# Key features of two token tiles by way of an SBUF copy, a third nested product in one mixing group, and new engine orders

## The chip, the cores and the metric

The kernel runs on one core of a Trainium2 chip. The metric is device time in microseconds (us) of one execution. Engines: TensorE (PE), which multiplies matrices; VectorE (DVE); ScalarE (ACT); GpSimd (POOL); SyncE (SP), which issues most of the DMA transfers. PE takes its operands from SBUF and writes PSUM, eight banks of 128 partitions x 512 fp32.

## The reference

The input is x of 2048 tokens x 512. The first part is linear attention over 32 heads of 16, the second a gated MLP with a spatial product over the tokens (F = 1792, Fh = 896):

```python
def _A_ref(x, wqkv, wo):
    qkv = ...            # x @ wqkv, split into 32 heads
    q, k, v = (qkv[0], qkv[1], qkv[2])
    phi = lambda t: jnp.where(t > 0, t + 1, jnp.exp(t)) + 1e-06
    pq, pk = (phi(q), phi(k))
    kv = jnp.einsum('bhsd,bhse->bhde', pk, v)
    z = jnp.einsum('bhsd->bhd', pk)
    num = jnp.einsum('bhqd,bhde->bhqe', pq, kv)
    den = jnp.einsum('bhqd,bhd->bhq', pq, z)[..., None] + 1e-06
    ...                  # (num / den) @ wo

def _B_ref(x, w_in, w_sp, b_sp, w_out):
    z = _gelu(jnp.einsum('bsd,df->bsf', x, w_in))
    z1 = z[..., :Fh].copy()
    z2 = _layernorm(z[..., Fh:], axis=-1)
    g = jnp.einsum('ts,bsf->btf', w_sp, z2) + b_sp[None, :, None]
    return jnp.einsum('bsf,fd->bsd', z1 * g, w_out)

h = x + _A_ref(_layernorm(x, axis=-1), A_wqkv, A_wo)
h2 = h + _B_ref(_layernorm(h, axis=-1), B_w_in, B_w_sp, B_b_sp, B_w_out)
```

## The kernel before

**Tiles and stages.** The 2048 tokens are 16 tiles of 128 rows. In the head (0 to about 46 us) each tile of x is normalised: BATCH_NORM statistics and their aggregation on DVE (L535, L536), or for tile 1 two accumulating passes on ACT; 1/sqrt(variance) by ACT (tiles 0, 2, 3) or POOL; then xn (L580 on DVE, L583 on ACT). For the first six tiles PE transposes xn (four transposes, L594) and ACT copies the result to xnT; the others are transposed by DMA. Four 512-wide matmuls by the key part of wqkv then give the keys of a tile in a PSUM bank, `phi` (L601) makes the key features pk, and L684 accumulates pk against xn over all tiles in four banks. From that sum follow the matrix m (cast at L794), and with the query features pqT the denominator (L817), its reciprocal r on ACT, the spread of r over partitions by DMA on SP (L808, `spread`), the multiply of pqT by r (L833), and the products pqT x m that give h (L845). Then come the second layer norm, w_in with gelu, the spatial mixing with w_sp, the gate and w_out.

**phi** takes exp of the keys on ACT (e), min and add on DVE (L606), and ends in one of two ways. Without `split` a DVE scalar_tensor_tensor (L611) reads PSUM: max(t + 1 + eps, e). With `split`, ACT copies t + 1 + eps to the destination in SBUF (bf16), and a DVE tensor_tensor (L609) takes the maximum there in place. For the keys, `k_unit` (L640) asks for each tile i below SINGLE = 4 whether i is in KSPLIT, and for later pairs whether their first tile is.

**The mixing.** All large products are in Strassen-Winograd form: w_sp and z2 are cut into 2 x 2 blocks, and sums of blocks take the place of an eighth of the products. `mix(ia, ib, nest)` (L1060) does two pairs of token tiles, (ia, ia + 8) and (ib, ib + 8), over one half of the features, 448 wide (HW). The four calls take the tiles of MIX = (0, 1, 2, 3, 7, 4, 5, 6) two by two; the third has the tiles 7/15 and 4/12. Set c uses the PSUM banks B = SETS[c], A = B + 1 and E = B + 2, with SETS = (0, 3); the banks 6 and 7 are left for other work, in this stage for `mo_pair`. `gate` (L1006) finishes a piece: ACT adds the bias out of PSUM into u (L1011), DVE multiplies z1 by u in place (L1012). `gate_p` (L1020) does it when a part p was set aside earlier: DVE adds PSUM and p into u (L1023), then multiplies (L1024). When a tile is finished, SP issues a transposing DMA of z1 to zgT, named zg and the tile number, which w_out needs.

**A nested product** (`nested`, L1035) takes a further level of the same scheme for both pairs of a group together: seven products of four matmuls, 224 wide (HQ), in two banks, with four sums u of the weight's quarters (L748, `comb`), four sums v of the other operand's quarters (`quarter_sums`, L1028), two adds of a piece p into PSUM (L1044) and four 224-wide copies on ACT (L1045). The same operand takes 2 x 8 matmuls of 448 without it. NEST gives each of the four groups a number: bit 1 nests the first product, bit 2 the product of q1 with zt1. The first group has neither, the others have both.

**w_out.** `mo_pair` (L1130) does it for two tiles, again in Strassen form, in two banks (6 and 7 for all but the last pair): sums us of zgT (L748), matmuls, adds of h into tmp (L1147) and the final adds into h (L1159), then a store. The last two tiles go through `mo` (L1122, add at L1127). `mo_pair(0)` runs from 139.9 us, between the second and third group's matmuls.

**Order.** Nothing is scheduled at run time. ORDER is a packed list of the numbers of all operations (1256), and each engine runs its own in that order and waits for semaphores where an operation depends on another engine or on a DMA. So an operation that has to wait holds everything that stands behind it on its engine. Buffers are placed by hand at byte offsets, and two tiles may share an address when their uses don't overlap; the dependencies include those.

Of the kernel before, what the change touches and what calls it, by code (L numbers as in the profile page):

```python
# [252 lines left out]
def bass_sequential_preLN__linear_attn_block__mixer_gmlp__prompt_kernel(  # L253
# [14 lines left out]
    H = 32  # L268
# [151 lines left out]
    def matmuls(out_ap, pairs, start=True, stop=True, onto=False, **k):  # L420
        n = out_ap.free_size() if callable(getattr(out_ap, "free_size", None)) else out_ap.shape[-1]

        kw = {"skip_group_check": True} if onto else {}

        def fn(pe):
            inst = None
            for i, (a, b) in enumerate(pairs):
                inst = pe.matmul(out_ap, lhsT=a, rhs=b, start=start and i == 0, stop=stop and i == len(pairs) - 1, **kw)  # L428
            return inst
        return PE(fn, [a for p in pairs for a in p], [out_ap], len(pairs) * max(65.0, n / 2.4 + 2.5), **k)  # L430
# [437 lines left out]
    def half(b):  # L868
        return bank(b, HW)
# [150 lines left out]
    def gate_p(n, c, b, p):  # L1020
        o, u = z1[n][:, c], u_t[cnt[0] % len(u_t)]
        cnt[0] += 1
        dve(lambda v: v.tensor_tensor(u, half(b), p, ALU.add), [half(b), p], [u], HW, ps=True)  # L1023
        dve(lambda v: v.tensor_tensor(o, u, o, ALU.mult), [u, o], [o], HW, acc=2)  # L1024
# [35 lines left out]
    def mix(ia, ib, nest, early=False):  # L1060
        ss = range(HT)
        sa = [[sae[0], sae[1]], [sae[2], sa_[1][1]]] if early else sa_
        sets = ((ia, 0), (ib, 1))
        Y = {}
        for i, c in sets:
            Y[i] = blocks(i)
        if nest & 1:
            nested(SETS[0] + 1, SETS[1] + 1, wt[ia][:, 0:HT, :], wt[ib][:, 0:HT, :], z2[:, 0:HT, lo], nu1, nv1, np1)
        for i, c in sets:
            B, A, E = SETS[c], SETS[c] + 1, SETS[c] + 2  # L1070
            y11, y21, y12, y22 = Y[i]
# [91 lines left out]
        load_w(n)  # L1163
    MIX = (0, 1, 2, 3, 7, 4, 5, 6)
    for k in range(0, HT, 2):
        mix(MIX[k], MIX[k + 1], NEST[k // 2], k == 0)
        if k == 0:
            for q in ZLATE:
                cell2(q, win1, wq1[0], 6, 7, p5z[q % 2], z1_half)
            load_wout()  # L1170
            for n in W4:
                load_w(n)
            if any(m & 1 for m in NEST):
                quarter_sums(nv1, z2[:, 0:HT, lo])
            if any(m & 2 for m in NEST):
                quarter_sums(nv5, zt1)
# [44 lines left out]
```

## Time and profile before

| | us |
|---|---|
| median of 3 executions (224.97 to 225.69) | 225.41 |
| the profiled execution | 225.59 |
| its span in the profile | 223.6 |
| PE busy, 1318 matmuls | 217.5 |
| DVE busy, 440 instructions | 191.3 |
| ACT busy, 271 instructions | 138.6 |
| POOL busy, 133 instructions | 46.6 |
| HBM read and written | 6.95 MB and 2.10 MB |

Busy times overlap; what matters is which engine the others wait for. The chain of waits is followed back from the last instruction, at each step to whatever released it. By its lines, 82% of the span is matmuls of L428, which is the helper for nearly all of them, and 6% those of L684. A group's line gives count, busy time and the mean of one; an instruction's time contains its start and drain, so a matmul's record overlaps the next one's, and the step from start to start is shorter than its duration. Line 2 of the page shows how full each of 40 slices of the span is; POOL is empty from the middle on:

```profile
PE   7799999998999999999999999999999999999995
DVE  3899778899999999999999998999695976694666
ACT  5587844469898999999674456624353434526130
POOL 2445400000279465637710000000000000000000
```

### The profile page before, as it was taken

The numbers are of one execution on the slowest core, as the hardware profiler recorded it, in microseconds if no ns is written. First come the engines' busy times: TensorE is split into PE (matmuls) and PEld (weight loads), VectorE is DVE, ScalarE is ACT, GpSimd is POOL, SyncE is SP. The second block draws the span as 40 slices with busy tenths as digits, with TensorE's granted clock in tenths as the row PEclk, the third lists the DMA queues.
The fourth block names the chain that finished last, engine by engine and source line by source line (L and its number), as shares of the span: only waits on it lengthen the run. The fifth ranks groups of instructions, "written<-read, shape, count | busy, mean of one in ns | idle before, by whom it ended". The sixth has DMA issues, their size and how long they took to land.

```text
span 223.6 us, 3752 instructions
## 1 busy us (share of the span) xinstructions
PE 217.5 (97%) x1318; PEld 121.6 (54%) x1318; DVE 191.3 (86%) x440; ACT 138.6 (62%) x271; POOL 46.6 (21%) x133
## 2 busy tenths in 40 slices
PE   7799999998999999999999999999999999999995
PEld 7344444443434545445555555767776658666664
DVE  3899778899999999999999998999695976694666
ACT  5587844469898999999674456624353434526130
POOL 2445400000279465637710000000000000000000
DMA  5664999977752359840843344998444208204444
GB/s 187 205 197 93 170 221 250 197 178 169 164 132 56 70 104 132 121 93 0 109 85 129 77 85 80 171 178 132 82 100 85 58 12 166 42 1 89 107 134 142
DMA packets 73938, 26.85 MB, mean 120 GB/s; under 512 B 63680, under 2 KB 73920, under 8 KB 73920
## 3 DMA queue, kind: packets, MB, share of 16 engines
q1 hardware_dynamic: 73216, 26.03, 56.7%
q10 hardware_dynamic: 704, 0.59, 0.8%
q8 instruction: 10, 0.16, 0.3%
q14 instruction: 8, 0.07, 0.1%
HBM read 6.95 MB, written 2.10 MB: 40 GB/s over the span
## 4 chain that ended last, share of the span: by engine, by line
PE 90%; DMA 4%; ACT 2%; DVE 2%; SPq 1%; ACTq 0%; issue 0%; DVEq 0%
PE psum L428 82%; PE psum L684 6%; DMA wqkv<-in_A_wqkv_dram 3%; DMA r<-rcp 1%; ACT ct L447 1%; DVE h L1159 1%; SPq L808 1%; DVE pqT L833 1%; PE psum L706 0%; PE psum L594 0%; ACTq L458 0%; DVE m L794 0%; ACT psum L447 0%; ACT r L447 0%; ACT z1t L447 0%
## 5 line engine op out<-in xcount | busy, mean ns | idle before, releaser
L447 ACT ACTIVATE psum<-psum 128x448 f32<-128x448 f32 (+2 forms) x67 | 28.0, 432 | 31.0 <-PE psum L428 24.3
L428 PE MATMUL psum<-z,wt 128*128 128x448 bf16 (+1 forms) x232 | 46.4, 343 | 0.1
L428 PEld LDWEIGHTS psum<-z,wt 128*128 128x128 bf16 x232 | 22.6, 98 | 17.7 <-ACT np L447 0.4
L428 PE MATMUL psum<-win,hnT 128*128 128x448 bf16 x112 | 25.8, 353 | 0.0
L447 ACT ACTIVATE e<-psum 128x1024 bf16<-128x1024 f32 (+1 forms) x18 | 16.7, 932 | 13.5 <-PE psum L428 13.5
L447 ACT ACTIVATE z1t<-psum 128x448 bf16<-128x448 f32 (+1 forms) x24 | 15.9, 669 | 4.6 <-PE psum L428 2.9
L428 PE MATMUL psum<-ws,hs 128*128 128x448 bf16 x72 | 18.7, 353 | 0.0
L447 ACT ACTIVATE p<-psum,b 128x448 f32<-128x448 f32 x16 | 9.8, 634 | 11.8 <-PE psum L428 9.7
L428 PEld LDWEIGHTS psum<-win,hnT 128*128 128x128 bf16 x112 | 10.7, 98 | 10.5 <-DMA hnT<-hn 0.4
L1023 DVE TENSOR_TENSOR u<-psum,p 128x448 bf16<-128x448 f32 x16 | 9.9, 621 | 7.5 <-PE psum L428 7.5
L428 PE MATMUL psum<-zt,sa 128*128 128x448 bf16 (+1 forms) x92 | 16.3, 316 | 0.0
L447 ACT ACTIVATE u<-psum,b 128x448 bf16<-128x448 f32 x16 | 10.1, 632 | 10.0 <-PE psum L428 8.8
L875 DVE TENSOR_TENSOR psum<-psum,p5z 128x448 f32<-128x448 f32 x24 | 14.9, 626 | 1.4 <-ACT z1t L447 0.4
L428 PE MATMUL psum<-wqkv,xnT 128*128 128x512 bf16 x64 | 15.3, 379 | 0.3 <-DMA wqkv<-in_A_wqkv_dram 0.2
L428 PE MATMUL psum<-xnT,wqkv 128*128 128x512 bf16 x64 | 15.3, 379 | 0.0
L684 PE MATMUL psum<-pk,xn 128*128 128x512 bf16 x64 | 15.3, 379 | 0.0
L428 PE MATMUL psum<-wout,zgT 128*128 128x256 bf16 (+1 forms) x77 | 15.1, 302 | 0.0
L428 PE MATMUL psum<-m,pqT 128*128 128x512 bf16 x64 | 14.7, 380 | 0.1
L447 ACT ACTIVATE z<-psum 128x896 bf16<-128x896 f32 x16 | 14.7, 918 | 0.1
L428 PE MATMUL psum<-zt,wt 128*128 128x448 bf16 x64 | 13.4, 352 | 0.0
L535 DVE BATCH_NORM_STATS2 st<-x 128x6 f32<-128x512 bf16 x15 | 9.8, 682 | 3.4 <-DMA x<-in_A_x_dram 3.3
L559 POOL TENSOR_SCALAR st<-st 128x1 f32<-128x1 f32 x10 | 3.7, 374 | 40.8 <-ACT sh L447 36.7
(153 smaller groups left out, 435.2 us busy)
## 6 DMA issues: line engine op xcount, KB each, us to landing
r<-rcp SPq DMA_DIRECT2D x16, 128.0 KB, 2.7
out_dram<-h SPq DMA_DIRECT2D x15, 128.0 KB, 1.8
win<-in_B_w_in_dram SPq DMA_DIRECT2D x4, 448.0 KB, 4.3
x<-in_A_x_dram SPq DMA_DIRECT2D x6, 256.0 KB, 4.3
wqkv<-in_A_wqkv_dram SPq DMA_DIRECT2D x2, 512.0 KB, 5.5
wout<-in_B_w_out_dram SPq DMA_DIRECT2D x1, 896.0 KB, 5.0
wt<-in_B_w_sp_dram SPq DMA_TRANSPOSE x32, 4.4
wo<-in_A_wo_dram SPq DMA_DIRECT2D x1, 512.0 KB, 4.6
```

Source lines behind the costliest of these rows:

```text
L428: inst = pe.matmul(out_ap, lhsT=a, rhs=b, start=start and i == 0, stop=stop and i == len(pairs) - 1, **kw)
L447: return g.add("ACT", lambda ac: ac.activation(out_ap, in_ap, func, **kw), [in_ap, *extra], [out_ap] + ([accum] if accum is not None else []),
L535: dve(lambda v: v.bn_stats(s[:, 0:6], src[:, n, :]), [src[:, n, :]], [s[:, 0:6]], D)
L559: pool(lambda p: p.tensor_scalar(s[:, 2:3], s[:, 0:1], s[:, 0:1], -1.0 / (n * n), op0=ALU.mult, op1=ALU.mult), [s[:, 0:1]], [s[:, 2:3]], 240)
L684: inst = pe.matmul(bank(CB[c]), lhsT=xn[:, i, c * P:(c + 1) * P], rhs=pk[:, i, :], start=i == 0, stop=i == NT - 1)
L808: g.add("SP", lambda q: q.dma_start(dst, src_ap), [rcp[:, i:i + w, :]], [dst], cost=700, lat=2200, dma=f"r{tg}{c // 2}")
L833: dve(lambda v, q=q, r=r: v.tensor_tensor(q, q, r, ALU.mult), [q, r], [q], 2 * GW, acc=2)
L875: dve(lambda v: v.tensor_tensor(half(b), half(src), p, ALU.add), [half(src), p], [half(b)], HW, ps=True)
L1023: dve(lambda v: v.tensor_tensor(u, half(b), p, ALU.add), [half(b), p], [u], HW, ps=True)
L1159: dve(lambda v, o=o, q=q, add=add: v.tensor_tensor(o, q, add, ALU.add), [q, add], [o], DH2, ps=True)
```

## The change

It does three things.

1. KSPLIT goes from empty to (0, 2): by the test in `k_unit`, tiles 0 and 2 take the `split` branch of `phi`. Each has one more ACT pass (PSUM to pk, 512 wide), and its DVE operation reads two bf16 tiles in SBUF instead of PSUM.
2. NEST goes from (0, 3, 3, 3) to (0, 3, 7, 3). Bit 4, new, nests a third product in the third group: the lower block of w_sp's row of `tl` by the second half of z2. It runs in the banks 6 and 7, and its results are gated from there with `gate_p`, with p2 copied out of bank A by ACT. Sums of z2's quarters (nv2) are made ahead of the group. The new buffers share addresses: nv2 with z1 of the tiles 2, 3, 10 and 11, nu2 and p2 with the tails of the w_sp rows 2, 10, 3 and 11.
3. ORDER is new, with 1279 operations. In the head, PE's transposes of the tiles 3 and 1 stand ahead of the first product by wqkv instead of behind it; ACT's second pass over tile 1 stands ahead of the first rstd pass, and DVE aggregates the tiles 2 and 3 ahead of the first xn. Between 18 and 40 us some loads change places on SP. In each of the first r spreads two issues change places, so that the part the first multiply waits for comes second of four. From about 139 us to the end, the order on PE, DVE, ACT and SP is new: `mo_pair(0)` starts behind the third nested product; the last two products of the last but one pair, and the order of transposes and stores on SP, change at the end.

```diff
-ORDER = "c-jTQ1Aq_!5Cp*8z00=o*)~7hwryLV`)u2`ZQHhO*9;I5kwC;pI7CJi7(&A#L`5`&L3G4J2qZuf#6Uvi...
+ORDER = "c-jTQ1Aq_!5Cp)z-OIM|*)~7hwryLV`)u2`ZQHhO*9;I5kzk0A(1?sE2nQh~98nPs;SmPW5f4NNBtR0xKt...
...
+    o_ur = [o_wsp + n * S * 2 + ZR for n in (2, HT + 2, 3, HT + 3)]
+    nv2 = [g.sbuf(f"nv2{k}", o_xnT + slot[n] * ZR, [HT // 2, HW // 2], BF16) for k, n in enumerate((2, 3, HT + 2, HT + 3))]
+    nu2 = [g.sbuf(f"nu2{k}", o_ur[k // 2] + k % 2 * (S // 2), [HT // 2, P], BF16) for k in range(4)]
+    p2 = [g.sbuf(f"p2{c}", o_ur[2 + c], [HW], FP32) for c in (0, 1)]
+    assert N4 <= ZR and ZR + S <= S * 2
...
-    QSPLIT, KSPLIT, CACT = (6, 7), (), 2
+    QSPLIT, KSPLIT, CACT = (6, 7), (0, 2), 2
...
-    NEST = (0, 3, 3, 3)
+    NEST = (0, 3, 7, 3)
...
             matmuls(half(B), [(q2[:, s, :], zt2[:, s, :]) for s in ss], **onto)
-            matmuls(half(A), [(wt[tl][:, HT + s, :], z2[:, HT + s, lo]) for s in ss], **onto)
-            gate(tl, lo, A)
+            if nest & 4:
+                act(p2[c], half(A), ACT.Identity, HW, bias=b32[:, tl:tl + 1], extra=[b32[:, tl:tl + 1]])
+                if c == 0:
+                    nested(6, 7, wt[ia][:, HT:NT, :], wt[ib][:, HT:NT, :], z2[:, HT:NT, lo], nu2, nv2, np1)
+                gate_p(tl, lo, 6 + c, p2[c])
+            else:
+                matmuls(half(A), [(wt[tl][:, HT + s, :], z2[:, HT + s, lo]) for s in ss], **onto)
+                gate(tl, lo, A)
...
     for k in range(0, HT, 2):
+        if NEST[k // 2] & 4 and not NEST[k // 2 - 1] & 4:
+            quarter_sums(nv2, z2[:, HT:NT, lo])
         mix(MIX[k], MIX[k + 1], NEST[k // 2], k == 0)
```

More of the change, by code (lines that the diff above doesn't have):

```diff
@@ L15 @@
 SEM_NS = 45.0
-ORDER = "c-jTQ1Aq_!5Cp*8z00=o*)~7hwryLV`)u2`ZQHhO*9;I5kwC;pI7CJi7(&A#L`5`&L3G4J2qZuf#6UviLSiIB0FojPQXv^~BQH`TIr1R|@*@pGq5x8&5DFqKVj=?q5epR&8-<Yx=};bVP!#DA7nM)}nNb9l(Fhq)1zAuGSy2^DPz{Zd15HsK+0YEx(HzB58#Pc0Ezlh;Q4_6@6D80Uwa^-+(FQ$G2i;H-J<$toQ3hpE7h}-}y-^OM(I55D4t+5IV=xZ&F&<&j9uv?Hi_rj+&;g;a6cf=9`#2fP&=E^82%Rt$%drAeFc62Z3gNL5BX9uI5QM`Rj<pz!XE=x<=!~a0f{}=TqgaP7SdCFQhT{mv44l9koWgXx!aU5xe4NBA%*IeGz+()<6D-6wF2V+^$7h_zS8T^de8F>U!zOIT9PGeL%*9T;#V+i|9(=<?yvG^r#aZmber&-xyu((U#|2!$4qnCwJi-lp!c|<vcHYD;Uc)8a!fjkfc>cp*#Nu~=cM+Q(aR-0!3vu`piFprk`2%DE2Jk+@F&@PvjL!!M!3Z=aV^W5sGc}Vl5+gDc!!RLJFe=k9ETb?q6EQ6#GcThtBU7>{(=#7qFax8rB8xE{W3n8Jb2n2lKeMnB>#_i|vOEj24YM(j^;m+HS(4eAnGINo6_|^e*q&RNlU3N3rC60YSegylkM&uNh1r3<S%i&Ph8;PQjoF9QS(Z)Mjy2eyquH08n1`J?fJfMrx%r((Igqv4jMF)agII?_?82HH%wW!9bB<vx&R|!L<uVT8Y|i93uH<r#=Nxw90iNIrPT(pY<3!%)K_2H_w&DXG=1I2ZJ@(`ep5kggVhjFcFCOA)uHjrh=0i^68D3_0w&WYm<514$6Q1Q2{$dsD!Kb{+zdXma{LSG!&ue_kbsWYEbS>aizT-mv;dLg^2wtT0o;R37>-moxXriVuo<ax;rOAB8><X<ZT*Q!yuO$qloZ8Gp`oKL*tgyPtDB8$d%&m`1sJsfNTnbQB6;d9BR}$@Ke%)po<x^69Vl-8?&+Mt^+{D6q!L;h3=z7Tldc`~3!gTt=UW%cDilBPB#6U$<AH~#CrdKTW)>p<>GG)+W7F7}TRWT)39YxY>WK?n0RUDPqYt~mo^-~I!&>J*RN;T3Bl~e^a)(Z?!YkgxARn$&ZQX9=vT<ua@_19o!(m)MTJ7rd7WzlX$R*+I@j;d&gN@<VgDyvFszS^sdhN-OfYN&>5p_(eS7HEVPX}qdxq_XL~s;QY4tGPaEf|jU-R;#5t=!iaOjYg@Xma3B`>XXVTSZmcvlhj$CwNJ}5T3_`=)pbIXwNA_RO$W6?D|J#+^j%}LUOzQfKQvW`v_aD}UB5I=f3%YuRYQlhNk=t9oAp~=^j8P8N?Y_#$3#0V*jd$-Y^!F<?3}vlf$nIQ+<xP(LRdGQ(iw%c<Eo`Fc0uVZl-02N3T@j|TVd^@9_zfq*=$9&OA2pSby*SYp04Pjwkx7N(ltF%B)hIC)?HEUsiIpnyP;=_Vb4|9vUp6psX`XpV%ZDb(rv}D+7{R1*-O>8_*TmjSpv&#ua(fMSz^m?uM}W!l*f`<5-VnJ)xh2<nH9H&mctuaaw}jZET!#b3Ttd7EtQqB!j{I;TWTw9b*!kBu_ji~(ppB#<4vuC)w9fA(VAIS%jzwyvK6ts-pblrUTbTaEYR|K8*67}t+{2h4wln9TW&9B`7Eckur4;i@_S9oZi}pkmA3+(*(O?R>uHs2fbCa7?`6HMx-GMgw$fHxMW14wEYJtqAS>j#yuanLu9n@`S~eeQMSZdLu^?MveXW}n_kOm@rrKaD<?F1x7xpE#!G>88A7az3m=Cv6HrdwO2%Bb;Y^1HRO;*xp+6>EJ8*P?V_RaRmN_Z77?ZGzBwp&@BZ4YdRjj=g4-zxY*dt|$;xtH;MR?e&XSgYn)th(>EN?z0FS`8m<Tdce7u?4o(_F64pYWwYg)%An+(4N?1tL@9}f}OW*cF2y|VH;;HeY}0KomStE+d2Ddjr^&dwG(#IzS(oD<5#Sq|Fp(F&|CW{`(^dKg*Wgc*2bIqMQh@1y}h^dj(*90*iCz8m+iOxu?~LPu39Va<Yz30b@pr4)w}o$yKXP7zaO>F*3Dm8cmHR%tcTw)_-muTvo|JxZ{|Jyj@>r*UjETSdqfZ8Z!Ns{^{IZ>26&K%^LsYf`*;YyZ&5vx5Al#b%!m3QAK}w{xX1F5zSbjq1YhT)J&KR=8UEcq*jSJ4UoDykdnixr8+?pM_i-NJ6FiPj@)$nZ<9bXV@4bDd$Mabp)@OSXPvmnwz9;lKp1{|8a-Z(=JgLw36u!V0drDvG3q6^q@l?LZmwReo;Y&QNPw{2G(O3H>Z|285y|40>p3XP>7T@aI{kUiFZGO~uct$_vC;YT$@_T;9&-yv<=R19k-}ei?%Xj+&Kks{eqF?kqzTfxxNx$R={Gng=!+y{Y`4xZUNBo*!^_%|Kulo&u;<x>l-|?q@*Pr=+a4v9b"
@@ new lines @@
+ORDER = "c-jTQ1Aq_!5Cp)z-OIM|*)~7hwryLV`)u2`ZQHhO*9;I5kzk0A(1?sE2nQh~98nPs;SmPW5f4NNBtR0xKtkk2QY1odBt|j>ARm$=4^kmNQlJ1*BP9wV4GJRy0uc&nQ3Qn$6X}ovv5+1W5gV0J3~`VNaZw3HQ3Xwq5mk`|)sPv@P#oD%9i@;JHP95zkrUZb6D^PfEl~n>Q43|z3MJ7Ut<eUxkqbRh2W?Rn?a&ML&;zB>8|Bak?NJ`%Q6K%#7h_QY12F;P&;T7U5&ba;lh6<yF$I$`9Rsi&jj$A*&=@nY3@b1dov{+DFc@7h4QmjD)mV=s7=;fwgdsSJkywkNc#dJ{il+$1I&{Nm9L5;T#4&8Zam>OAoWwJP#X`)+3oO7X%)wj?$0D4@2%N!UEWt*c#U^~j8+^r1Y{n<-z-K(h7VNNj*oCc_k0;oTz1V~I*oQAThws>rZ#a*gb^r&l4Hxhl+i?+>a1AeU6?^O!u49*7#%<id72LsH+(bk(gT=8Q_=o$5Yd>)hv_FVvzmdcqAin*AEP*AphlpT_%q^KEv_}YGkt~!Yw-grILRwl&X;Cb(g|Tp!%A#9jOK0INnuWChOK(vvzs0bOmfDJ21}k8(ER)5w%2vWMTWqUfB`u8=v}{(z>RX^?w~AKCN?AM0VGXRbRkFgC$Ff)>D`HhGr?t0^*3fcWHOp$%t&HWe##X}ySXnD-O{|mkwPLp2np!z)X2Dj|`dN9aWu0xHjkV_1!SY!PJ7)bYuXVAXHpuGQOdD<WEXc-LR~ut<teds8+IHM#Sshzp<882Yx4AakCfI5_WJ7GP^{{!i(oWeLn{TV^p-r>}cES$ZBzt5-?Y_0Kg?7?TTW@P?5A3M@vNN{Up4e~eV`puhJ+)!>*v{DzduEfZm94j{Hqtg&YkO`}?44b+Keo|&+Id@K;C1U|!|kuVw;OiB7TZ({$r1L?rrQU*X`3t&Kbo_eF4`!|MPmrwvIGpp8778dLgr*xzA!R0r`a+K$K2d%0sLf17@qrVvqj@)%ge;f&j`%J+m@7f?2<)i5$0n=CgVX{Vs|Ya3o<zi@Uq3=7wgUH`f6LOC|_E7_Tnpx$=4RhH@400SqAoDA;#i2Yrrd3n333z%PlrDGBW!z4!>Ip#^qAW#NsT*{w%?itj8#Pi_9#^`i#eld}|Ham;;!KrT7kwn3_$vi=|nKO?kiuu`PdCGgjtqzCsnY;{wL#9=7K|4&{E!!XOT22WDkeX5(H)<q)RfJXYf{mf=3mXLgq5LUv?1j$nE2=WveXVm4=5F5)OI;Y3zvFmv!DYp?~EvL!!r5|^<R*RnM`@fbgG9Y?b>m$M5e^9w6*4A-*_r?4x(@&H$GEWh&`Yw{GQasyZL2M==<SMxNd@h8V|BY$%|e{njGa1&>6CjW2(|8ci%W-T7&79Qs;ZslKgBXo#sxQ(V0l+Kbm&)Rft=WK@11$O5n-s2pG)L-0ZDD~hOo?~d8WF3anC1y|<)zU+T)ehEWcwOdGUStH#WmH{ZL|x}qM$!Xb<74h*WIf>xK4TQ!WHj|;bUkNG#n3IjU@X04eU<Xqy3Hbrt2lbaJG{$ys;l@)pw~RehDxY93Q!{D)mtW34JA=Qy<t+lV?HHUGL_JKHqr;CP)RjbId7trs^F!RT7k-;RBEcyN~1C=s&vYtv?{B5Dz0*Brb0@uY^tQ@YM_&<tQKnFRn=M<RZJ~aSRGYcnbk%e)J~n$O6`?Z`PEe`R9<bBQx()p6*W)=)LEG{NVC*iRkTXoR8!N`Mdf|E2CKW)Xr^W>NJF$<8`VP_v{^khR9n<n!!$?3RnfC+hURLmwrReODz`?ck4pP-t<yY>)M#zeR*ljE_0uE;YoS(Zhx%)~255|yXs1qTk&bDX7Hh2bDvx$+nNDk;#%YfZYN;k`xu)oh4(ouvYrIZqf)44dChCUvYqicPqQB5x<x*HbqVsyH=enmSD&s$NS<m!aS9C$wbW<1gQ?E5um-I)sbXEUU$^YuMD*JWC@Rx!|ar2T+f1_qz#Up!F@8>oAm*mwvq&N5bs_voufol3&x%c;$9?oNW9gpg<yq=f!THe4vsJ1ushZ^9q{gJ}>E7kSK`lz^G-=ldPZ{n@IvB&e)9^OBzjkoo79^Kn}GVkDte2RDU`2IzSy^DwN1m4X*sgn=%<le(OdqPj@U)9rlc~|f5gZz$qduV^BAn)TT{F?@Q5+CYAJhi{qa3AIwe1tdkk)F{5e3S?K8js*(e6)}Au|Cz)_;{b_lRT17_8C6YbNejM;j?{?r}VWx*VFnupYEAGmCyGhp53Q;PG97iJc}>zCBD$JdM;n)*?hUD^L4(#k9s4|=Zig$Z}jxO)C>74U+J5Cv*-6Mp4SWedf(;+e5)7ryT08EdJzxw<9^R~croAQ6a2p4@jbrNANoGu?fd<a7x%q>%pdy+FX0FMq#yFH{=iT9Q$OIR{fw{hbN<B7`fC5?&-}a}_UC@V`}zyN<QM&=fA=f?%3u36f9u!%jlcJIe#0;O2fyl{{D*(^&wkUt_;0`EKmE4<@n8Pe{{tUYhMW"
```

## The prediction

> **What bounds the kernel.** I read the page first, for the busy shares and the chain of work that ended last.
>
> ```profile
> PE 217.5 (97%) x1318; PEld 121.6 (54%) x1318; DVE 191.3 (86%) x440; ACT 138.6 (62%) x271; POOL 46.6 (21%) x133
> PE 90%; DMA 4%; ACT 2%; DVE 2%; SPq 1%; ACTq 0%; issue 0%; DVEq 0%
> ```
>
> TensorE (PE) carries the end: 90% of the chain, and VectorE (DVE) with 86% is close behind. So a change gains by taking matmul time out or by closing a gap in front of a matmul, and it loses by making DVE late. Next the chain in order of time, for where it leaves PE.
>
> ```profile
> 1.71 5.89 DMA wqkv<-in_A_wqkv_dram
> ...
> 50.96 2.70 DMA r<-rcp
> 53.69 0.59 DVE pqT L833
> ...
> 140.99 72.65 PE psum L428 x496
> 213.72 6.06 PE psum L428 x44
> 219.80 1.42 DVE h L1159 x4
> ```
>
> There are two such places that the change touches: the start, where PE waits for the last half of wqkv, and 50.96, where the spread of r by DMA holds a multiply at 53.69 and the products at 55.64. From 140.99 on PE never waits. The busy time by stage shows how much room the other engines have there (columns: PE, weight loads, DVE, ACT, POOL, clock, DMA share, GB/s).
>
> ```profile
> 7.74:14.91 7.17, 7.13 (x44) 3.37 (x45) 7.11 (x21) 5.38 (x11) 2.33 (x6) 1.00 0.74 224
> 14.91:46.42 31.51, 31.51 (x157) 14.04 (x158) 27.25 (x48) 17.67 (x21) 6.53 (x20) 1.00 0.88 178
> 139.50:172.00 32.50, 32.49 (x230) 22.29 (x231) 28.11 (x70) 15.37 (x36) 0.00 (x0) 1.00 0.76 130
> 172.00:207.00 35.00, 35.00 (x238) 22.96 (x237) 24.92 (x68) 14.84 (x34) 0.00 (x0) 1.00 0.29 60
> ```
>
> The granted clock is 1.00 in each, so a matmul costs the same everywhere. PE is full; DVE is full in the head (7.11 of 7.17) and at 86% (28.11 of 32.50) where the third nested product comes in.
>
> **Part 1, the key features.** The list KSPLIT is tested only for tiles below SINGLE = 4, tile by tile, so (0, 2) reaches tiles 0 and 2 and no others. For each, DVE's 512-wide L611 is replaced.
>
> ```profile
> L611 DVE SCALAR_TENSOR_TENSOR pk<-psum,e 128x512 bf16<-128x512 f32 x4 | 2.6, 674 | 0.0
> L748 DVE TENSOR_TENSOR nu<-wt,wt 128x512 bf16<-128x512 bf16 x3 | 1.2, 416 | 0.0
> ```
>
> The new maximum over two bf16 tiles of 512 elements is not in the trace in this place; the nearest row is the 512-wide L748, 0.42 us. So DVE saves 2 x (0.67 - 0.42) = 0.5 us. ACT gets two 512-wide passes out of PSUM, some 0.60 each like its other 512-wide pass there (597 ns), 1.2 in all; it has 7.17 - 5.38 = 1.79 idle between 7.74 and 14.91, 1.13 of it in two waits for PE (0.64 before 11.01, 0.49 before 12.10). Neither is on the path by itself: the cost is nothing as long as these idle stretches take it, and at most 0.2 if the copies of xnT behind it (due at 12.69 and 14.86, each with 0.05 us to spare) are pushed back.
>
> **Part 2, the order of the head.** PE's own records:
>
> ```profile
> 7.10 0.40 PE L594 MATMUL psum<-ident,xn 128*128 128x128 bf16 x4 [0.78 <-DVE xn L580]
> 7.74 1.02 PE L428 MATMUL psum<-wqkv,xnT 128*128 128x512 bf16 x4 [0.24 <-DMA wqkv<-in_A_wqkv_dram]
> 8.60 0.61 PE L594 MATMUL psum<-ident,xn 128*128 128x128 bf16 x8
> 9.04 2.79 PE L428 MATMUL psum<-wqkv,xnT 128*128 128x512 bf16 x12
> ```
>
> The eight transposes at 8.60 (tiles 3 and 1, 0.22 us each group, 9.04 - 8.60 in all) now stand ahead of the product at 7.74. VectorE's two aggregations move ahead of tile 0's xn, which brings the rstd pass of tiles 2 and 3 from 6.06 to about 5.75 and the transposes at 7.10 to 6.85; the squares of tile 1 go ahead of tile 0's rstd on ACT, and xn of tile 1 comes at about 7.15 instead of 7.51. The last transposes then run from 7.62 to 7.85, and the product starts at 7.85 instead of 7.74. Four 512-wide matmuls are 8.60 - 7.74 = 0.86, so the next product starts at 8.71 instead of 9.04: -0.33. Behind it PE has one gap (0.20 before 14.91) and then none to 46.42, so what is gained at 14.91 is carried; the stretch needs DVE 0.3 earlier as well, which the 0.5 of part 1 pays for. Bounds: -0.4 (the gap before 14.91 shrinks too) and 0 (loads or ACT eat it). I take -0.3, near the worked end, since each step has a row.
>
> **Part 3, the spread of r.** The first r pair now completes at the second of its DMA issues on SP instead of the third, 0.60 earlier by the chain's issue steps (0.68 and 0.60). The multiply at 53.69 could start at 53.2, when its other input is there; the products at 55.64 then depend on the cast of m and the second multiply, in the DVE queue: I get 55.46. Bounds 0 and -0.5; I take -0.2.
>
> **Part 4, the nested product.** In the group of tiles 7/15 and 4/12, 2 x 8 matmuls 448 wide go, and 7 x 4 matmuls 224 wide come.
>
> ```profile
> 143.82 3.38 PE L428 MATMUL psum<-z,wt 128*128 128x448 bf16 x17
> ...
> 150.97 0.55 PE L428 MATMUL psum<-z,wt 128*128 128x224 bf16 x4
> ```
>
> The last matmul of a run is shown with its drain (352 and 259 ns). So one 448-wide is (3.38 - 0.352) / 16 = 0.189 us; four 224-wide run from 150.97 to 151.35, when the next matmul starts, 0.38 or 0.095 each, up to 0.097 elsewhere. Out: 16 x 0.189 = 3.02. In: 28 x 0.096 = 2.69. Net -0.33.
>
> The price stands on DVE:
>
> ```profile
> L748 DVE TENSOR_TENSOR nv<-z 128x896 bf16<-128x896 bf16 x1 | 0.6, 614 | 0.0
> ...
> L1044 DVE TENSOR_TENSOR psum<-psum,np 128x224 f32<-128x224 f32 x12 | 4.5, 392 | 2.3 <-PE psum L428 2.3
> L1023 DVE TENSOR_TENSOR u<-psum,p 128x448 bf16<-128x448 f32 x12 | 7.5, 621 | 6.5 <-PE psum L428 6.5
> ```
>
> Four sums nv2 (0.61), four sums nu2 (0.42), two PSUM adds (0.39), two adds of p2 (0.62): 2.46 + 1.66 + 0.78 + 1.24 = 6.1 busy. DVE's instructions overlap by some 0.08 us, so its queue grows by about 5.1. ACT gets four 224-wide copies, 4 x 0.35 = 1.4; its passes for p2 replace those for u. Cover: DVE has 32.5 - 28.1 = 4.4 idle up to 172, and the whole mo_pair(0) moves behind 172 (2 adds of 0.42 into tmp, 4 into h of 0.42 and about four sums us of 0.35, 3.9 in all), since its banks 6 and 7 are now the nested product's. That makes 28.1 + 6.1 - 3.9 = 30.3 busy of 32.2, 94%; counted without the overlaps less. Behind 172 DVE has 35.0 - 24.9 = 10.1 to take mo_pair(0). Walking DVE's new list against PE's, I find each input of a matmul in time, the closest ones by 0.03 us (the first sums, near 144.5) and 0.5 us (the add into Y1 near 171.3, which the next product on that bank waits for). In DVE's queue stand the nv2 sums, and behind them the u sums and gate adds that free PSUM banks for PE. They write into z1 of tiles 2, 3, 10 and 11, so each waits until the zg transpose of that tile has been read out:
>
> ```profile
> DMA to landing us min/median/max: 2.9/2.9/4.7
> ```
>
> At 2.9 us those of tiles 3 and 10 land 1.3 and 0.6 us before their sums' turns. I take 0 for the waits; the other end is below, with the rivals. The tail (the last two pieces of the last pair moved ahead of the last mo, other store order) ends as before: last matmul, DVE add, one store.
>
> **Sum.** -0.3 - 0.2 - 0.33 = -0.83. The profiled execution took 225.59 (span 223.6 and 2.0 around it), so 224.8 for one like it; it lay 0.18 above the median 225.41, so the forecast on the median is **224.6 us**. Its own range, from the bounds above: with -0.4 - 0.5 - 0.33 it is 224.2, with the head at 0 and r at 0 it is 225.1; and 0.2 for small waits or gains that I don't see: 224.0 to 225.2.
>
> **Rivals.** (That the change does less than its list of tiles seems to say is settled by the code: two tiles, and the sum counts two.)
>
> *Half hidden.* The gain of the head is lost because ACT's two extra passes delay the xnT copies, which have 0.05 us to spare, or r's earlier multiply meets the cast of m. For it: those slacks; against it: ACT idles 1.13 just there. Only part 4 and a part of the others remain: 225.41 - 0.33 - 0.1 = 225.0.
>
> *Weight loads bind.* Narrow matmuls get no cheaper than the loads of their weights.
>
> ```profile
> L428 PEld LDWEIGHTS psum<-nv,nu x72: 96/98/99, 135.6 to 192.8; 128*128 128x128 bf16 x72
> ```
>
> At 98 ns each, 28 x 0.098 = 2.74, the saving is 0.28 instead of 0.33; were the loads 107 ns, 28 x 0.107 = 3.0 and nothing is saved: 225.41 - 0.5 = 224.9. The trace has the 224-wide matmuls at 95 to 97 ns, so little chance. (The Trainium skill, "TensorE: Matmul & The Clock Gate", section "LDWEIGHTS (loading the stationary operand)", gives columns / 1.2 ns, an estimate of 107 ns for 128 columns, whatever the contraction: by it a split to 224 columns would be worth nothing. The rows here, 98 ns for the load, speak against it by a tenth.)
>
> *DVE becomes the bound, slower.* One mechanism: the nv2 sums stand in DVE's queue behind the zg transposes of tiles 2, 3, 10 and 11, which all pass SP's one queue. If tile 10's landing takes the 4.7 us that the trace shows at most, 1.8 more than the median, its sum starts 1.8 - 0.6 = 1.2 late, and with it everything behind it on DVE: the u sums, the gate adds, the add into Y1. If tile 3's, just ahead in that queue, is as late and the two add up, it is 3.0. DVE at 94% can't make that up before 172, and mo_pair(0) is no longer there as PE's filler, so PE waits as long: 225.41 - 0.83 + 1.2 to 3.0 = 225.8 to 227.6. Near the lower end, since at least half of the landings are at 2.9, I price it at 226.3. It ends above the time before from a lateness of 0.83 on. For it: the DMA share of 0.76 in that stretch and DVE's load; against: a median landing equal to the shortest.
>
> **How the numbers follow.** Chances: forecast 0.58, half hidden 0.15, weight loads 0.06, DVE late 0.21. A measurement of this kernel tells no less than 0.3% from no change, 0.68 us: faster is below 224.73, slower above 226.09. Of the forecast 0.50 lies below 224.73 and 0.08 within; of half hidden 0.03 and 0.12; weight loads 0.06 within; of DVE late 0.04 within and 0.17 above. That is faster 0.53, same 0.30, slower 0.17. The range leaves out less than 0.05 below 223.9 and some 0.13 above 226.3, the price of the slower case.
>
> **What would show it.** In the head, the product now at 9.04 starts near 8.7 and the one at 14.91 near 14.6. The r multiply starts near 53.2, the products at 55.64 near 55.2 with the head's gain. The 28 new matmuls show about 96 ns from start to start. PE stays at 32.5 of 32.5 from 139 to 172, DVE above 90% there. The forecast is wrong if PE shows a wait on a DVE sum or add between 140 and 175 (then the third rival), if weight loads appear as what PE waits for, or if a gap opens in the head behind an xnT copy (the first).

## The result and the profile after

| | us | executions |
|---|---|---|
| changed kernel, median (range) | 224.98 (224.20 to 226.16) | 22 |
| kernel before, beside it | 225.59 (224.97 to 226.0) | 22 |
| profiled execution of the changed kernel | 225.66, span 223.9 | 1 |

The ratio is 0.9973 with a 95% interval of 0.9963 to 0.9982: faster by 0.27%, 0.61 us. Two more measurements of the same kernel, further down, give 0.9951 and 0.9969. Note that the profiled execution is 0.7 above the median, so its span says nothing of the gain; it has to be read place by place.

The page of the changed kernel, busy times and chain:

```profile
PE 218.1 (97%) x1330; PEld 123.0 (55%) x1330; DVE 195.4 (87%) x452; ACT 140.9 (63%) x277; POOL 47.9 (21%) x133
PE 72%; ACT 12%; DMA 6%; DVE 5%; POOL 2%; issue 1%; SPq 1%
```

There are twelve matmuls, twelve DVE instructions and six ACT instructions more, as counted from the code. PE's share of the chain falls from 90% to 72% though PE is as busy as before: the chain is followed from wait to wait, and two waits lead it off PE for long stretches. One is for the DMA transpose shown below (PE resumes at 32.10), the other for a DVE add at 93.56, from which the chain goes back over POOL, ACT and DVE to 65.8. Without the first it is 79% (a_again and pre_only, below), and 91% and 92% in the two runs that also mend the second (mid_fix and mid_and_load). The same four stages as shown of before (columns PE, weight loads, DVE, ACT, POOL, clock, DMA share, GB/s):

```profile
7.74:14.91 7.17, 7.05 (x41) 3.13 (x39) 6.67 (x21) 6.56 (x13) 2.43 (x6) 1.00 0.72 224
14.91:46.42 31.51, 30.99 (x154) 13.52 (x155) 26.32 (x44) 17.77 (x21) 6.03 (x17) 1.00 0.92 176
139.50:172.00 32.50, 32.45 (x228) 21.75 (x228) 29.26 (x69) 17.41 (x40) 0.00 (x0) 1.00 0.69 126
172.00:207.00 35.00, 35.00 (x251) 24.24 (x250) 27.67 (x76) 13.54 (x33) 0.00 (x0) 1.00 0.22 49
```

In the head DVE has lost 0.44 and ACT gained 1.18, as the two split tiles should give. In the stage of the nested product DVE is at 90% (29.26 of 32.50) and PE is still full. The loss is in the second line, where PE was full before: 0.52 is missing. PE's records of the head, and then those of that place:

```profile
6.83 1.11 PE L599 MATMUL psum<-ident,xn 128*128 128x128 bf16 x12 [0.32 <-DVE xn L585]
7.78 3.62 PE L433 MATMUL psum<-wqkv,xnT 128*128 128x512 bf16 x16
...
14.83 1.04 PE L433 MATMUL psum<-wqkv,xnT 128*128 128x512 bf16 x4
```

```profile
29.70 1.89 PE L689 MATMUL psum<-pk,xn 128*128 128x512 bf16 x8
32.10 1.67 PE L433 MATMUL psum<-wqkv,xnT 128*128 128x512 bf16 x7 [0.51 <-DMA xnT<-xn]
```

All twelve transposes stand ahead of the first product by wqkv now, and sixteen matmuls run in one piece. At 32.10 PE waits for the DMA transpose of xn of tile 12 (issued at 25.36, landed at 31.96, 6.6 us; transposes of xn that meet no large load take 2.5). Counted from start to start, 0.67 us are lost. Set beside the first profile of before, PE's start of the same work shifts as follows: -0.40 at the second key product (9.04 before), -0.08 at the product behind the head (14.91), +0.77 behind this wait, +0.60 at the products by m, +0.40 at 79 us, +0.70 at 139.51 and +0.30 at the last product. So two places that the forecast named, the spread of r (-0.17) and the nested product (-0.40), gave about what it said, and the head gave 0.08 of its 0.3. Places that it did not name took more than all of that in this execution: 0.85 in transposes that landed late (0.67 here, 0.17 near 18 us), and 0.30 between 79 and 139.5 us; 0.20 came back between the products by m and 79 us. The runs below ask which of these losses belong to the change and which to the execution.

### The profile page after: what moved, and what is told of

The parts are those of the page before. It is cut to its first block, busy times and chain, and to the rows that moved or that the text cites. A ratio compares the mean times of both kernels' runs of the same rounds, so it can differ in the third digit from the quotient of the medians.

```text
span 223.9 us, 3802 instructions
## 1 busy us (share of the span) xinstructions
PE 218.1 (97%) x1330; PEld 123.0 (55%) x1330; DVE 195.4 (87%) x452; ACT 140.9 (63%) x277; POOL 47.9 (21%) x133
## 4 chain that ended last, share of the span: by engine, by line
PE 72%; ACT 12%; DMA 6%; DVE 5%; POOL 2%; issue 1%; SPq 1%
PE psum L433 67%; PE psum L689 4%; DMA xnT<-xn 3%; DMA x<-in_A_x_dram 3%; ACT z L452 2%; DVE h L850 2%; ACT e L452 1%; ACT z1t L452 1%; ACT sq L452 1%; DVE st L540 1%; ACT ct L452 1%; ACT psum L452 1%; POOL rs L548 1%; ACT p5z L452 1%; ACT xn L452 1%
## 5 line engine op out<-in xcount | busy, mean ns | idle before, releaser
L452 ACT ACTIVATE psum<-psum 128x448 f32<-128x448 f32 (+2 forms) x70 | 29.0, 428 | 39.7 <-PE psum L433 32.1
L433 PE MATMUL psum<-z,wt 128*128 128x448 bf16 (+1 forms) x224 | 44.0, 339 | 0.1
L433 PEld LDWEIGHTS psum<-z,wt 128*128 128x128 bf16 x224 | 21.8, 98 | 16.5 <-ACT np L452 0.4
L1028 DVE TENSOR_TENSOR u<-psum,p 128x448 bf16<-128x448 f32 x18 | 11.2, 621 | 4.7 <-PE psum L433 4.7
L452 ACT ACTIVATE z<-psum 128x896 bf16<-128x896 f32 x16 | 14.7, 923 | 0.3 <-PE psum L433 0.2
L433 PE MATMUL psum<-wout,zgT 128*128 128x256 bf16 (+1 forms) x77 | 14.7, 302 | 0.0
L433 PE MATMUL psum<-m,pqT 128*128 128x512 bf16 x64 | 14.7, 380 | 0.0
L452 ACT ACTIVATE u<-psum,b 128x448 bf16<-128x448 f32 x14 | 8.9, 633 | 8.8 <-PE psum L433 8.8
L433 PEld LDWEIGHTS psum<-zt,sa 128*128 128x128 bf16 x92 | 8.9, 98 | 5.7 <-ACT psum L452 0.4
L452 ACT ACTIVATE p<-psum,b 128x448 f32<-128x448 f32 x18 | 11.0, 638 | 1.5 <-DVE psum L1049 1.5
```

Source lines behind the costliest of these rows:

```text
L452: return g.add("ACT", lambda ac: ac.activation(out_ap, in_ap, func, **kw), [in_ap, *extra], [out_ap] + ([accum] if accum is not None else []),
```

## The experiments

All change only what is named; the other orders are those of the kernel they start from. "The changed kernel" is the one of the result.

**The changed kernel again (a_again, a_third), and the kernel before again (b_again).**

> The changed kernel once more, for a second profiled execution. In the first one PE waits 0.67 us at 31.4 for a transpose of xn (issued 25.36, landed 31.96) and ends 0.30 us later than the one of before, though the median is 0.6 lower. Theory 'sporadic': that wait is in some executions only; here it is under 0.3 and the span about 223.0. Rival 'built in': the two win loads issued just ahead of that transpose always hold it; the wait is again 0.5 to 0.8. Ratio to before in both cases 0.996 to 0.9985.

> The changed kernel on the chip of the next two, to compare them with, and a third profiled execution of it. Ratio to before 0.995 to 0.9975. From the product at 140 us to the last one 80.23 us as in its two other profiles (80.63 before), and from the last r product's matmuls to the first by m 2.73 (2.90 before); the head between 14.49 and 14.85, the earlier the sooner x of tiles 4 and 5 lands.

> The kernel before, unchanged, for a second profiled execution of its head. In the first one the last half of wqkv landed at 7.60 us, its first product started at 7.74 and the product behind the head at 14.91, 7.17 later. Theory 'the gain hangs on the loads': that product starts 7.1 to 7.2 us behind the first one, and the first one 0.14 behind the landing, though not ahead of 7.5, where the transposes end. If the landing is at 7.0 to 7.2 as in some executions of the changed kernel, it is 14.7 against 14.44 to 14.52 there, a gain of 0.2 to 0.25 us; with a landing at 7.6 it is 14.9 or more again. Rival: 14.9 or more with an early landing too, then the gain is the 0.4 that the two first profiles of either kernel show.

a_again: 224.61 us (6 executions), ratio 0.9951 (0.9935 to 0.9966), profiled at 224.40 with a span of 222.7. (The ratios are taken against the kernel before as it ran beside each measurement.) The product that waited runs on:

```profile
29.17 1.89 PE L689 MATMUL psum<-pk,xn 128*128 128x512 bf16 x8
30.90 1.89 PE L433 MATMUL psum<-wqkv,xnT 128*128 128x512 bf16 x8
```

The transpose landed at 30.14, 0.76 us ahead of its product. a_third: 225.11 us (12), ratio 0.9969 (0.9943 to 0.9995); there it came late again, by 0.44, and the next one by 0.18. So the wait comes and goes, with a margin that is too small for how DMA times vary. Of the ten profiled executions that have this order of loads, three show it (0.67, 0.61 in two waits, 0.20), 0.15 us on the average; the three with the loads in the order of before don't. That the new order causes it is not shown by this. In the old order, too, two w_in loads stand 1 us ahead of that transpose, and its margins there are 0.95, 1.18 and 1.08 us; in the seven profiles of the new order without the wait they are 0.76 to 1.96. What the three late ones have in common is slow w_in loads (4.8 to 6.1 us). Transposes of xn come late at another place in either order (0.53 near 18.5 us in tail_only, 0.75 near 17.3 in mid_fix).

b_again was profiled once (225.79 beside 225.9). With it, three heads of the old order and several of the new one can be compared where the first loads landed alike:

| order of the head | run | wqkv complete | x of tiles 4, 5 | product behind the head |
|---|---|---|---|---|
| before | before | 7.60 | 7.92 | 14.91 |
| before | tail_only | 7.68 | 8.23 | 15.09 |
| before | b_again | 7.14 | 7.75 | 14.86 |
| changed | changed kernel | 7.61 | 8.18 | 14.83 |
| changed | zg10_late | 7.44 | 8.00 | 14.64 |
| changed | pre_only | 7.15 | 7.71 | 14.52 |
| changed | a_again | 6.99 | 7.36 | 14.49 |

In pairs with like landings the gain is 0.34 (b_again and pre_only), 0.27 (before and zg10_late) and 0.26 (tail_only and the changed kernel). The first two profiles show only 0.08; x landed 0.26 later in the second of them. The expectation that the old head would come at 14.7 with early loads was wrong: it came at 14.86, nearer to the rival's 14.9. a_third's head came at 15.47, outside what was expected: x of tiles 2 and 3 landed there at 5.12 and 5.29 instead of 4.1 and 4.2, and everything behind it started one us late.

**The two halves alone (tail_only, pre_only).** tail_only has the third nested product and the new orders behind 139 us, pre_only has everything ahead of them.

```diff
 tail_only
-    QSPLIT, KSPLIT, CACT = (6, 7), (0, 2), 2
+    QSPLIT, KSPLIT, CACT = (6, 7), (), 2
     # ORDER ahead of 139 us as in the kernel before
 pre_only
-    NEST = (0, 3, 7, 3)
+    NEST = (0, 3, 3, 3)
     # ORDER behind 139 us as in the kernel before
```

> The third nested product with the new order behind 139 us, everything ahead of it as before. By the prediction's sum it is worth -0.33 us, ratio 0.9985. Theory 'tail carries it': the whole gain sits here, ratio 0.997 to 0.998. Rival 'DVE late': the extra DVE work makes PE wait, ratio 1.000 or more.

> All that the change does ahead of 139 us (the split key features, the orders of head, loads and r spread), the rest as before. The prediction's sum gives -0.5 us, ratio 0.9978. Theory 'given back': the head's 0.4 is lost again by 14.9 us because x of tiles 4 and 5 lands no earlier, only the 0.17 of r stays: ratio 0.999 to 1.000. If the transposes that land late are built in, it is 1.001 to 1.002.

tail_only: 225.08 us, 0.9979 (0.9964 to 0.9994). pre_only: 225.22 us, 0.9978 (0.9967 to 0.999). Each half is worth some 0.2%, and together they make the 0.9957 that lies between the three measurements of the whole (0.9951, 0.9969, 0.9973): neither theory that puts all of it into one half holds, and neither half is a loss. pre_only also contains what the section on the change does not list: between some 20 and 100 us, DVE, ACT and POOL, and PE in a few places, run in another order too. The trace is sharper than the times here. From the first product at 139.51 to the first of the last seven matmuls (220.14 before) it is 80.63 us in the kernel before and in pre_only, and 80.23 in the changed kernel, a_again and tail_only: 0.40 in each, whatever the loads did. For r, from the product ahead of the first spread's multiply (53.21 before) to the products by m it is 2.43 before and 2.26 in a_again, pre_only and the changed kernel, 0.17 less. DVE of a_again, where the multiply now stands ahead of the min and add that it followed:

```profile
52.17 0.68 DVE L799 CAST m<-psum 128x512 bf16<-128x512 f32 x1
52.77 0.68 DVE L838 TENSOR_TENSOR pqT<-pqT,r 128x1024 bf16<-128x1024 bf16 x1
53.37 0.42 DVE L611 TENSOR_SCALAR e<-e 128x1024 bf16<-128x1024 bf16 x1
```

**The split of the key features (no_ksplit, ksplit4).** The changed kernel without it, and with it for all four tiles that are done singly.

```diff
 no_ksplit
-    QSPLIT, KSPLIT, CACT = (6, 7), (0, 2), 2
+    QSPLIT, KSPLIT, CACT = (6, 7), (), 2
 ksplit4
-    QSPLIT, KSPLIT, CACT = (6, 7), (0, 2), 2
+    QSPLIT, KSPLIT, CACT = (6, 7), (0, 1, 2, 3), 2
     # ORDER, ACT: each new pass behind the exp of its tile
```

> The changed kernel without the split for tiles 0 and 2, its orders kept. Theory 'ACT pays': without the two extra passes ACT's xn of tile 7 comes 0.2 earlier, the wait of 0.17 at 18.3 goes, and the time is the same or 0.1 to 0.2 less (0.9990 to 1.0000 of the changed kernel). Rival 'DVE relief carries the head': DVE needs the 0.5 us in the head, the product at 11.45 and all behind come 0.2 to 0.4 later, ratio to the changed kernel 1.001 to 1.002.

> The changed kernel with the split for all four single tiles, two more 512-wide passes on ACT right behind their exps, DVE's order as it is. DVE saves another 0.5 us in the head, ACT pays 1.0 to 1.2 in a stretch where it is busy 6.25 of 6.86 us. Theory 'ACT is full now': the copies of xnT for tiles 4 and 5 come 0.3 to 0.6 late and PE with them, ratio to the changed kernel 1.001 to 1.003. Rival 'DVE is still what counts': 0.9985 to 1.000.

no_ksplit: 225.32 us, 0.998 (0.9969 to 0.9991); ksplit4: 226.3 us, 1.0014 (0.9989 to 1.004), beside 0.9969 of a_third on the same chip. So two tiles are better than none, by a_again on the same chip as no_ksplit, whose interval ends just below that of no_ksplit (those of the other two measurements of the changed kernel overlap it); and four are worse than two, where the intervals touch. Without the split the product behind the head starts at 14.76, with loads that landed as in pre_only (14.52): 0.24 later. Of this, 0.07 is there at the first product already (7.90 against 7.83), and no run explains it. The reason for the rest is not the one expected: the transposes of tile 4 wait for the PSUM bank that tile 0's keys stand in, and without the split DVE reads it late. DVE, then PE of no_ksplit:

```profile
10.77 0.68 DVE L616 SCALAR_TENSOR_TENSOR pk<-psum,e 128x512 bf16<-128x512 f32 x1
```

```profile
11.51 0.40 PE L599 MATMUL psum<-ident,xn 128*128 128x128 bf16 x4
```

The read ends at 11.45 and the transposes start at 11.51. With the split ACT has read the bank by 10.56 (pre_only) and the transposes run at 11.29. The theory that ACT pays for it (a wait of 0.17 at 18.3 us in the first profile) fell: a_again has the split and not that wait. With four tiles ACT pays indeed; its copy of xnT is what PE then waits for, and DVE's saving bought nothing. (In this execution x of tiles 4 and 5 landed late as well, at 8.34, and a transpose held PE for 0.20, so not all of its long time is ACT's.)

```profile
15.74 0.60 PE L433 MATMUL psum<-wqkv,xnT 128*128 128x512 bf16 x2 [0.61 <-ACT xnT L452]
```

**How far DVE is from being the bound (zg10_late, dve_pad4).** One makes the sum of nv2 wait for its DMA, the other adds four sums to DVE's queue at the same place.

```diff
 zg10_late: ORDER, SP
-    zg3, zg10, wt14 (second half), zg11
+    zg3, wt14 (second half), zg10, zg11
 dve_pad4
             quarter_sums(nv2, z2[:, HT:NT, lo])
+            for _ in range(4):
+                comb(nv2[2], z2[:, HT + H4:NT, HQ:HW], z2[:, HT:HT + H4, HQ:HW], ALU.subtract)
```

> The changed kernel with the transpose of tile 10 issued one place later on SP, behind a w_sp load: it lands about 1.3 us later, 163.4 instead of 162.15, where its sum of nv2 has its turn at 162.44. The prediction's rival 'DVE late': PE loses what the sum is late, 1.0 us, ratio to the changed kernel 1.004. Theory 'slack behind': DVE's idle of 0.18, 0.28 and 0.60 us between 163.7 and 167.1 takes it up, the product that needs this sum comes only at 169.15; PE waits less than 0.2, ratio within 1.001.

> The changed kernel with four further copies of the third sum of nv2 on DVE, each 0.53 us of its queue, 2.1 in all, at 162.4. It measures how far DVE is from being the bound. Theory: its idle up to 167.1 takes 1.06, the add into Y1 at 170.85 (0.19 us ahead of its product) comes 1.06 late, PE waits 0.8 to 0.9 before 173 and the end comes as much later: ratio to the changed kernel 1.0035 to 1.004. If DVE were far from the bound, nothing; if it were at it, as the prediction's 94% would have it, 1.9 or more, 1.0085.

zg10_late: 224.65 us, 0.9956 (0.9936 to 0.9976), no slower than a_again or a_third. DVE's wait is there, a whole 1.15 us, and PE's products of the nested multiplication behind it follow one another as closely as ever. From the product at 140.63 in the changed kernel to the last matmul it is 80.46 us in the changed kernel, in a_again and here.

```profile
163.97 0.62 DVE L753 TENSOR_TENSOR nv<-z 128x896 bf16<-128x896 bf16 x1 [1.15 <-DMA zgT<-z1t]
```

```profile
171.34 0.55 PE L433 MATMUL psum<-nv,nu 128*128 128x224 bf16 x4
171.73 0.55 PE L433 MATMUL psum<-nv,wt 128*128 128x224 bf16 x4
172.11 0.49 PE L433 MATMUL psum<-wout,zgT 128*128 128x256 bf16 x3
```

dve_pad4: 226.07 us, 1.0022 (1.001 to 1.0034), slower than the changed kernel by a good 0.5%. The added sums show in one row of five, and PE waits for the add into the PSUM bank that comes last in that queue:

```profile
163.02 3.26 DVE L753 TENSOR_TENSOR nv<-z 128x896 bf16<-128x896 bf16 x5
166.20 0.42 DVE L753 TENSOR_TENSOR nu<-wt 128x512 bf16<-128x512 bf16 x1
172.75 0.39 DVE L1049 TENSOR_TENSOR psum<-psum,np 128x224 f32<-128x224 f32 x1
```

```profile
173.20 0.56 PE L433 MATMUL psum<-nv,wt 128*128 128x224 bf16 x4 [1.02 <-DVE psum L1049]
```

The five sums take 3.18 us up to the next instruction (166.20 - 163.02) where one takes 0.53 in a_again. So 2.65 us were added, and not the 2.1 expected: the copies write the same buffer, and they start 0.66 us apart. They cost PE 1.18 us from start to start (1.02 in this wait). That is more than the 0.8 to 0.9 expected from 2.1, and far from all of it. About 1.5 us of slack (2.65 - 1.18) is left in that stage, which a DVE share of 90% does not tell by itself. The changed kernel was not run on that chip; the half per cent compares ratios.

**A step of DVE's order in the middle (mid_fix).** All profiles of the new order have a longer wait near 92 us. In a_again, DVE and then PE:

```profile
90.68 0.51 DVE L585 TENSOR_SCALAR z<-z,st,rs 128x896 bf16<-128x896 bf16 x1 [0.49 <-POOL rs L548]
91.10 0.62 DVE L950 BATCH_NORM_STATS2 st<-z 128x6 f32<-128x448 bf16 x1
91.64 0.61 DVE L880 TENSOR_TENSOR psum<-psum,p5z 128x448 f32<-128x448 f32 x1
```

```profile
92.31 0.55 PE L433 MATMUL psum<-win,hs 128*128 128x448 bf16 x2 [0.30 <-DVE psum L880]
```

DVE idles for POOL's rstd with an instruction whose result no matmul waits for at once; the add into PSUM stands behind it, and PE waits for the add.

```diff
 mid_fix: ORDER, DVE
-    z2 normalised (L585), statistics (L950), add into PSUM (L880)
+    statistics (L950), add into PSUM (L880), z2 normalised (L585)
```

> The changed kernel with one step of DVE's order moved: the normalising of a half of z2 that waits for POOL's rstd at 90.2 (0.49 us idle) goes behind the PSUM add that PE waits for at 91.9. Theory 'queued behind a wait': the add starts when its matmuls are done, 91.3 instead of 91.6, PE's wait ahead of the product at 92.3 shrinks from 0.47 to about 0.13 as in the kernel before, and all behind it comes 0.3 earlier: 0.9985 of the changed kernel, some 0.995 of the one before. Rival 'POOL's rstd is what is late for everybody': the wait moves to the next product, nothing gained.

mid_fix: 224.47 us (8), 0.9954 (0.9937 to 0.9971). The add starts when its matmuls end, the normalising comes after it without a wait, and PE's lost time goes from 0.47 to 0.13:

```profile
92.23 0.63 DVE L880 TENSOR_TENSOR psum<-psum,p5z 128x448 f32<-128x448 f32 x1 [0.23 <-PE psum L433]
92.77 0.50 DVE L585 TENSOR_SCALAR z<-z,st,rs 128x896 bf16<-128x896 bf16 x1
```

That wait is mended, as the trace shows. Not all of it stays: a wait of 0.09 at 97.5, which the changed kernel had lost, is back. From the products by m to the first product `nv,nu` (135.18 in a_again) PE gains 0.29 on a_again. By the times alone, whose interval overlaps that of the changed kernel, nothing would be shown.

**Loads (x4_early, mid_and_load).** x4_early asks for x of tiles 4 and 5 ahead of the first half of wqkv; mid_and_load is mid_fix with a w_sp load put behind the w_in loads.

```diff
 x4_early: ORDER, SP
-    x0, x2, wqkv (first half), x4
+    x0, x2, x4, wqkv (first half)
 mid_and_load: mid_fix, and ORDER, SP
-    xn transpose 10, w_sp 9, w_in, w_in, xn transposes 12 and 13, w_in, w_in
+    xn transpose 10, w_in, w_in, xn transposes 12 and 13, w_in, w_in, w_sp 9
```

> The changed kernel with x of tiles 4 and 5 asked for ahead of the first half of wqkv instead of behind it. Theory 'x4 sets the head': it lands 0.4 to 0.7 us earlier, the transposes of tile 4 never wait, and the product that started at 14.49 to 14.83 starts by 14.5 also in executions with slow loads; the first product by wqkv stays near 7.8, because the transposes ahead of it end only there: 0 to 0.3 us less, 0.9985 to 1.000 of the changed kernel. Rival 'wqkv sets it': that half lands as much later, the first product starts after 8.1 and 0.3 or more is lost.

> The changed kernel with the moved step of DVE's order (worth 0.33 us in the profile) and with one w_sp load on SP (issued 22.5) put behind the four w_in loads, so that less is in flight ahead of the transpose of xn that came late by 0.67 once. Theory: that transpose is issued 1.3 us earlier and lands a good 1.5 us ahead of its product instead of 0.76; the wait at 31.4 is seen in no execution, ratio to the changed kernel 0.998 to 0.9985. Rival: the load comes in the way of the transposes of tiles 14 and 15 instead, 0.9985 to 1.000.

x4_early: 225.0 us, 0.9974 (0.9954 to 0.9994). x landed at 6.99 and the product behind the head started at 14.53 though wqkv was complete only at 7.75, so the mechanism is as expected; but nothing is gained in the time. Its profile has a wait of 0.53 at 66.3 for a transpose of hn; b_again, the kernel before, has one of 0.47 at the same place, so it isn't put down to this order of loads. mid_and_load: 224.64 us, 0.9952 (0.9926 to 0.9978), beside 225.11 of the changed kernel on the same chip, 0.47 less where 0.33 + 0.15 was to be expected from the two waits (0.29 for the first, by the profile). Its profiled execution took 224.06, the fastest profile of the study. The transpose was issued at 24.17 and landed at 28.80, 2.0 us ahead of its product:

```profile
29.12 1.89 PE L689 MATMUL psum<-pk,xn 128*128 128x512 bf16 x8
30.85 1.89 PE L433 MATMUL psum<-wqkv,xnT 128*128 128x512 bf16 x8
```

It is the fastest of the three on its chip, but its interval and that of a_third overlap, and mid_fix and a_again have lower medians (224.47 and 224.61) on other chips. No best version can be named from these times.

## Why the prediction came out right

The forecast was 224.6 us, 0.81 under the median it was made against; measured are 0.61 less at first, and 0.98 and 0.58 in the two repetitions by medians (0.61, 1.1 and 0.7 by the ratios). The direction holds, and the size within some three tenths. But 0.61 lies under the 0.68 from which on the prediction called it faster, so in the outcome "same" to which it gave 0.30, though the measured interval leaves out no change; and 224.98 is also the 225.0 of its half hidden rival. So the time alone does not decide between the two, and the terms in the trace have to. They bear the sum out for its named terms. Point by point:

**The head, -0.3.** It is -0.26 to -0.34 where the loads are alike. The mechanism is as put: the first product starts at 7.78 in the changed kernel instead of 7.74 (7.80 and 7.83 in a_again and pre_only, 7.62 to 8.78 over all runs), with all transposes ahead of it, and the second one at 8.64 instead of 9.04, 0.40 earlier, a little more than the 0.33 worked out. What was not seen is that x of tiles 4 and 5 sets the next transposes: when it lands at 8.18, 0.22 + 0.10 of the 0.40 go again at 11 us. That the split of the key features is needed for it is shown by no_ksplit (0.24 later, some 0.16 of it by the bank that the split frees and not by DVE's 0.5 us); that ACT has room for two tiles and no more, by ksplit4.

**The spread of r, -0.2.** -0.17 in each profile.

**The nested product, -0.33.** The whole stage gives -0.40 in each profile. The 28 matmuls run at 0.096 us from start to start (four from 171.34 to 171.73 above): 2.69 in, 3.02 out, as worked out. The remaining 0.07 are three things that the step did not count: two small waits at 140.5 and 142 us (0.03 and 0.12), and a 64-wide matmul near the end that held the next product for 0.24 before and 0.02 now. PE of before, then of the changed kernel:

```profile
213.48 0.19 PE L1184 MATMUL psum<-wout,zgT 128*128 128x64 bf16 x1
213.72 0.50 PE L428 MATMUL psum<-wout,zgT 128*128 128x256 bf16 x3
...
211.93 0.19 PE L1197 MATMUL psum<-wout,zgT 128*128 128x64 bf16 x1
211.95 0.71 PE L433 MATMUL psum<-wout,zgT 128*128 128x512 bf16 x4
```

The rival by which weight loads bind is out. The Trainium skill's rule in "TensorE: Matmul & The Clock Gate", section "LDWEIGHTS (loading the stationary operand)", would give an estimate of 0.107 us for each load of 128 columns; the trace disagrees with 0.096 from one of these matmuls to the next, and 0.098 for a load.

**The slower rival, DVE late.** Its margins were nearly right (0.3 us for tile 10 instead of 0.6, 1.2 for tile 3 instead of 1.3, from the landings and sums of a_again), and so was DVE's load (90% instead of the 94% counted without overlaps). Its price was wrong. "DVE at 94% can't make that up before 172, and mo_pair(0) is no longer there as PE's filler, so PE waits as long" fell with zg10_late: 1.15 us late on DVE, nothing on PE. The idle stretches behind that sum (0.18, 0.28 and 0.60 between 163.7 and 167.1 in a_again) lie ahead of the instruction that PE waits for, and the product of the late sum starts five and a half us after the sum does. Its upper end is not refuted: by dve_pad4, where 2.65 us cost 1.18, a lateness of 3.0 would cost some 1.5 (an estimate). No profile here had two transposes as late as that. A chance of 0.21 was more than these runs bear out.

**The half hidden rival.** Its reason, the two ACT passes, is not what hides anything. But some of the gain is hidden, and elsewhere: in stretches that the forecast did not price. The transpose of tile 12 comes late in three profiles of ten, 0.15 us on the average; whether this belongs to the changed order of loads or to slow loads in these executions is not shown. And the new order between 67 and 97 us drops four waits of PE (0.10 - 0.03, 0.05, 0.21 and 0.08 of before), has a new one of 0.13 near 76 us and lengthens one (0.13 to 0.47): 0.05 lost on balance, and 0.24 gained in mid_fix, where that one is mended.

So the terms in the trace are -0.3 (head), -0.17, +0.05 (from the products by m to 139.5), and -0.40: -0.82 in all, or -0.67 if the +0.15 for the transposes is the change's, beside 0.61, 0.98 and 0.58 measured. That the named terms add up so close to 0.83 is in part luck: the 0.07 that nobody counted in the last stage makes up for the 0.05 lost in the middle and for a little of r. What is left open: whether the late transposes are the change's, and whether the 0.98 of a_again, from six executions, is more than the scatter of the loads. The new order of the last 30 us was not run by itself.

## What to carry to other kernels

Price each reordered DMA by the margin between its landing and the instruction that needs it, and by what is issued just ahead of it: here a transpose whose margin was some 1 us missed it in three profiles of ten. An engine's share of a stage doesn't say what lateness costs: look for its idle stretches between the late instruction and the first one that the bounding engine waits for. And where an instruction waits for a slow helper, whatever urgent stands behind it in the same queue should go first.

## What the runs showed of the hardware

The same program's first loads land at quite different times: x of tiles 2 and 3 at 3.87 and 4.18 us in a_again and at 5.12 and 5.29 in a_third, the last half of wqkv between 6.99 and 7.78. The product behind the head starts at 14.49 in a_again and at 15.47 in a_third, 1 us apart. A DMA transpose of 128 x 512 elements takes 2.5 us by itself, 3.7 to 5.3 behind two loads of 448 KB in most profiles, and 5.3 to 6.6 in the changed kernel's first one, in a_third and in ksplit4; the loads themselves took 4.8 to 6.1 there instead of 3.9 and 4.5 in a_again. Sums of 896 bf16 elements on DVE start 0.53 us apart when each writes a buffer of its own, and 0.66 apart in dve_pad4, where they write the same one.
